# Moving the last quarter of an output product behind the next group's first tiles, in a fused attention and MLP kernel

## The chip, the cores and the metric

The kernel runs on one core of a Trainium2 chip. The time is that of the device in microseconds for one execution; the figure for a kernel is the median of several. A core has four compute engines with queues of their own, each of which runs its instructions in order: TensorE (PE in the profile), VectorE (DVE), ScalarE (ACT) and GpSimd (POOL). SP is a queue that only starts transfers. An instruction waits on semaphores that other engines and transfers raise; while it waits, everything queued behind it on its engine waits too.

## The reference

There are 8 batches of 8 heads, with 576 rows of 64 elements in each of q, k and v. k and v are averaged over 8 rows at a time, so that 72 remain; attention is then computed with all 576 rows of q. The result, 4608 rows of 512, goes through two matrices with a shrinking function between:

```
k_p, v_p = mean of k, v over groups of 8 rows
attn     = softmax(q @ k_p^T / 8) @ v_p          per batch and head
x        = attn, heads side by side              4608 x 512
h        = x @ w_in                              512 -> 2048
out      = (h - tanh(h)) @ w_out                 2048 -> 512
```

## The kernel before, in words

The order of every engine's work is written out by hand; the queues get their instructions in the order of the program's lines. PSUM, where TensorE puts its results, is addressed as eight banks of 512 fp32 values a partition, and `bank(i, shape)` names one of them. `Banks` is a rotation over some of them; a bank that is given out again makes its writer wait until the last reader has finished.

The rows are worked off in nine groups of 512. Groups 0 to 7 take the first 512 rows of each batch, group 8 the last 64 rows of all eight. For each group TensorE makes 16 tiles of h, each from four matmuls of 128x512 over `w1b`. ScalarE takes tanh of a tile into `TS`, and VectorE subtracts it and writes `Gt`. Group 0 handles tiles one by one (`mlp_h`, L580 to L582). Later groups handle tiles p and p + 8 as a pair in two neighbouring banks (`h_pair`, L616 to L622): eight matmuls, one tanh of 128x1024 at L621, one subtraction at L622.

The second product differs too. Group 0 multiplies straightforwardly (`mlp_o`, L586 to L603). For each of four row blocks `tb` it runs over the 16 tiles in four quarters `qd`, in the order of the tiles `W2_ORDER = (0, 8, 4, 12)`; after the last quarter ScalarE copies the bank to `O` (L601) and SP stores two blocks at a time. Groups 1 to 8 use a scheme with seven half-size products (`product`, L665) on sums of the blocks of `Gt` (`sum_p`, `sum_q`, `sum_d` on VectorE, L630, L635 and L640) and on sums of the blocks of `w_out`. These weight sums (`w_sum`, L648, and two ScalarE multiplications by −1 at L1015) are made once, in halves of the 8 tiles, during group 0. One of them, `b12`, is changed in place, so its half can only be made after group 0 has read those rows of `w2b`.

While group 0's output product runs, batch 1 is prepared: GpSimd adds the rows of k (`pool_k`, L247 and L252), VectorE makes `kd` (L259). TensorE turns k and q by a product with the identity (L328, L216) and makes the scores (L374), ScalarE exponentiates them (L389, L406, L407). TensorE multiplies by the values (`av_mms`, L463), VectorE divides, and TensorE turns the result into `xT` (L542). VectorE sums the rows of v and spreads them into `VB` (L270 to L309). These steps stand in a loop over 16 steps `u`, one `mlp_o` call each. Its score and turn banks rotate over banks 5, 6 and 7.

Batch 2 and later are prepared during the h tiles of the group before. GpSimd pools k and v; SP turns kd and q by transposing transfers (`k_dma_transpose`, `q_dma_transpose`, L202 and L207), and GpSimd places k (`k_place`, L360 to L362). `v_spread` copies the pooled v by three transfers. Inputs two batches ahead are loaded by SP after that.

Loads of `w2b` are issued on GpSimd's queue (L742)[...]. `after(loads, x)` adds a dependency by hand: the load of batch 2's k waits for a w2 load this way.

Of the kernel before, what the change touches and what calls it, by code (L numbers as in the profile page):

```python
# [8 lines left out]
FP32 = mybir.dt.float32  # L9
# [34 lines left out]
def kernel(  # L44
# [192 lines left out]
    def halves(n, b):  # L237
        return ((0, n),) if b < 2 else ((0, n // 2), (n // 2, n))

    def pool_k(b, eng, t0=0, t1=NT, mid=(), last=None, dep2=None):  # L240
        r = k_raw[b % 2].rearrange("p t (j d) -> p t j d", d=D)[:, t0:t1, :, :]
        if b not in kdups:
            kdups[b] = work.tile([128, NT, 2, D], BF16, name="kd", tag="kd", bufs=1)
        kd = kdups[b][:, t0:t1, :, :]
        n = t1 - t0
        for ta, tb in halves(n, b):
            eng.tensor_tensor(  # L247
                out=r[:, ta:tb, 0:4, :], in0=r[:, ta:tb, 0:4, :], in1=r[:, ta:tb, 4:8, :], op=ALU.add
            )
        for i, m in mid[0:2]:  # L250
            load_w2(i, m)
        second = eng.tensor_tensor(  # L252
            out=r[:, :, 0:2, :], in0=r[:, :, 0:2, :], in1=r[:, :, 2:4, :], op=ALU.add
        )
        if dep2 is not None:
            after([second], dep2)
        for i, m in mid[2:]:
            load_w2(i, m)
        kd_done = (last or eng).tensor_tensor(  # L259
            out=kd,  # L260
            in0=r[:, :, 0:1, :].to_broadcast([128, n, 2, D]),
            in1=r[:, :, 1:2, :].to_broadcast([128, n, 2, D]),
            op=ALU.add,
        )
        return kd_done

    def pool_v(b, eng):
        r = v_raw[b % 2].rearrange("p t (j d) -> p t j d", d=D)
        for ta, tb in halves(NT, b):
            eng.tensor_tensor(  # L270
                out=r[:, ta:tb, 0:4, :], in0=r[:, ta:tb, 0:4, :], in1=r[:, ta:tb, 4:8, :], op=ALU.add
            )
        eng.tensor_tensor(
            out=r[:, :, 0:2, :], in0=r[:, :, 0:2, :], in1=r[:, :, 2:4, :], op=ALU.add
        )
        if b < 2:
            eng.tensor_tensor(
                out=r[:, :, 0, :], in0=r[:, :, 0, :], in1=r[:, :, 1, :], op=ALU.add
            )
            v_main(VB[b % 2], r[:, :, 0:1, :], eng, 0, NM)  # L280
            return v_left(VB[b % 2], r[:, NM, 0:1, :], eng)
        if b < 4:
            eng.memset(VB[b % 2][0:G, 0:H, D:D1], float(POOL))
        vps[b] = work.tile([128, NT, D], BF16, name="vp", tag="vp", bufs=1)
        return eng.tensor_tensor(
            out=vps[b][:, :, :], in0=r[:, :, 0, :], in1=r[:, :, 1, :], op=ALU.add
        )

    vps = {}

    def v_spread(b):
        vp, vb = vps.pop(b), VB[b % 2]
        nc.sync.dma_start(out=vb[0:G, 0:H:2, 0:D], in_=vp[0:G, 0:NM, :])
        nc.sync.dma_start(out=vb[0 : 128 - G, 1:H:2, 0:D], in_=vp[G:128, 0:NM, :])
        nc.sync.dma_start(out=vb[128 - G : G, 1:H:2, 0:D], in_=vp[0 : NM * LO, NM, :])

    def v_main(vb, vs, eng, t0, t1):
        n = t1 - t0
        eng.tensor_tensor(
            out=vb[:, 2 * t0 : 2 * t1, 0:D].rearrange("p (t s) d -> p t s d", s=2),  # L300
            in0=vs[:, t0:t1, :, :].to_broadcast([128, n, 2, D]),
            in1=mask[:, 2 * t0 : 2 * t1, :]
# [280 lines left out]

    o_tiles = {}

    def mlp_o(g, tb, qd, gts, pool=None, k0=0, k1=4):  # L586
        if qd == 0:
            p, tag = pool or (ps_o, "o_ps")
            o_tiles[tb] = p.tile([128, DM], FP32, name="o_ps", tag=tag)
        o_ps = o_tiles[tb]  # L590
        i0 = W2_ORDER[qd]
        for i in range(i0 + k0, i0 + k1):
            nc.tensor.matmul(  # L593
                o_ps[:, :],
                lhsT=gts[i][:, tb * 128 : (tb + 1) * 128],
# [345 lines left out]
    ps_h.n = ps_o.n = 0  # L941
    nc.scalar.copy(out=q_bf[:QT, R, :, :], in_=t0[:QT, :, R, :])
    load_q(1, False)
    load_main(v_pairs, v_raw[1], 1, 0, NM)
    load_q_tail(1, q_raws[1], nc.scalar)
    for i in range(5):
        mlp_h_mms(0, i, 2, 4)
# [1 line left out]


    for i in range(5, NHID):
        mlp_h(0, i, gts, bank((0, 1, 2, 3, 4, 0, 1, 2, 3, 4, 2)[i - 5], [128, TG]))
        if i == 7:
            q_pe_tail(0)
        if i == 9:
            scores_tail(0)
        if i == 11:
            ps_a.n = 0
            av(0, 4, ps_any, True)
            x_dma_transpose(0, 2)  # L960
    kd1 = pool_k(1, nc.gpsimd, mid=((4, 2), (6, 2), (12, 4)), last=nc.vector)
    after([w_sum(w2s[:, 3, :, :], b21, b11, ALU.subtract, nc.gpsimd, k, k + 2) for k in (0, 2)], kd1)
    after(load_k(2), w2_dmas[3])
    load_v(2)

    def q1_cast(t, h):
        nc.scalar.copy(  # L967
            out=q_bf[:, 0:R, h : h + 4, :].rearrange("p j h d -> p h j d"),
            in_=t[:, h : h + 4, 0:R, :],
        )  # L970

    o_pools = [(ps_o, "o_ps"), (ps_o, "o_ps"), (ps_h, "hT_ps"), (ps_h, "hT_ps")]
    pend = []
    for u in range(16):
        qd, tb = u // 4, u % 4
        if u == 8:
            scores_wide(1, (3,))
            scores_ends(1)
        if qd == 2:
            for t2 in (2 * (tb % 2), 2 * (tb % 2) + 1):  # L980
                mlp_o(0, t2, qd, gts, o_pools[t2], tb // 2 * 2, tb // 2 * 2 + 2)
        else:
            mlp_o(0, tb, qd, gts, o_pools[tb])
        if u == 0:
            q1 = q_raws.pop(1)
            q1_cast(q1, 0)
        if u == 3:
            k_transpose(1, ps_any, (nc.vector.tensor_copy, nc.vector.tensor_copy))
        if u == 4:
            q_pe_transpose(1, (0, 1), "act")  # L990
            q1_cast(q1, 4)
            nc.scalar.copy(out=q_bf[:QT, R, :, :], in_=q1[:QT, :, R, :])
            load_q(2)
            w_sum(w2s[:, 1, :, :], b11, b12, ALU.add, k1=4)
            w_sum(w2s[:, 0, :, :], b11, b22, ALU.add, k1=4)
            w_sum(w2s[:, 2, :, :], b21, b22, ALU.add, k1=4)
            w_sum(b12, b22, b12, ALU.subtract, k1=4)
            v1_done = pool_v(1, nc.vector)
            after(
                [  # L1000
                    w_sum(w2s[:, 3, :, :], b21, b11, ALU.subtract, nc.gpsimd, k, k + 2)
                    for k in (4, 6)
                ],
                v1_done,
            )
            w_sum(w2s[:, 1, :, :], b11, b12, ALU.add, k0=4)
        if u in (5, 6):
            q_pe_transpose(1, (u - 3,), "act")
        if 5 <= u <= 7:
            scores_wide(1, (u - 5,))  # L1010
        if u == 6:
            q_pe_tail(1)
        if u in (9, 11):
            n = (u - 9) // 2
            nc.scalar.mul(  # L1015
                out=w2s[:, 4, 4 * n : 4 * n + 4, :], in_=b22[:, 4 * n : 4 * n + 4, :], mul=-1.0
            )
        if 11 <= u <= 14:
            x_pe_transpose(1, *pend.pop(0))
        if 9 <= u <= 12:  # L1020
            pend.append((u - 9, av(1, u - 9, ps_any, False)))
        if u == 13:
            w_sum(w2s[:, 0, :, :], b11, b22, ALU.add, k0=4)
            sums = w_sum(w2s[:, 2, :, :], b21, b22, ALU.add, k0=4)
        if u == 15:
            ps_a.n = 0
            av(1, 4, ps_any, True)
    pool_k(2, nc.gpsimd, dep2=sums)
    pool_v(2, nc.gpsimd)
    w_sum(b12, b22, b12, ALU.subtract, k0=4)  # L1030

    for g in range(1, NG):
        nb = g + 1 if g + 1 < B else None
        nn = g + 2 if g + 2 < B else None
        for p in range(NP - 1):
            c = p if g > 1 else p - 2
            if nb is not None and 0 <= c < 3:
                q_cast_part(nb, c)
            h_pair(g, p, ((2, 0, 4, 6, 0, 2, 4) if g == 1 else (0, 2, 4, 6, 0, 2, 4))[p], p % 2)
            if 3 <= p < 6:  # L1040
                sum_p(2 * p - 6, 2 * p - 4)
            if nb is not None and p == 0:
                k_dma_transpose(nb)
            if g == 1 and p == 0:
                x_dma_transpose(1, 2)
            if g > 1 and p == 0:
                store(g - 1, 2, 4, nc.gpsimd)
                store(g - 1, 0, 2, nc.gpsimd)
            if nb is not None and p == 0:
                k_place(nb, nc.gpsimd.tensor_copy)  # L1050
            if nb is not None and 0 <= c < 3:
                q_dma_transpose(nb, c)
            if nb is not None and c == 2:
                v_spread(nb)
                if nn is not None:
                    load_k(nn)
                    load_v(nn)
                    load_q(nn)
        h_one(g, NP - 1, 1, 0, 2)
        h_one(g, NP - 1, 0, 1, 3)  # L1060
        sum_p(6, 8)
        sum_q(0, 4)
        sum_q(4, 8)
        if nb is not None:
            sum_d(0, 2)
            sum_d(2, 4)
        ps_a = Banks(2, 3, 4, 5, 0, 1)
        for u in range(14):
            n, half = u // 2, u % 2
            bk, lhs, rhs = products[n]  # L1070
# [57 lines left out]
```

The softmax here doesn't subtract the row's maximum and nothing guards it: scores larger than these inputs give would overflow.

## Time and profile before

| | before |
|---|---|
| median of 8 runs | 285.69 us (285.26 to 286.61) |
| the profiled execution | 285.26 us |
| its span in the profile | 283.4 us |
| PE busy | 276.2 us, 97% |
| VectorE busy | 223.2 us, 79% |
| ScalarE busy | 157.9 us, 56% |
| GpSimd busy | 114.6 us, 40% |
| chain of waits | PE 93%, transfers 2% |

The span runs from the first to the last instruction of the profile. Where a stage is spoken of by its time, that is microseconds from the span's start. A row of the timeline shows the start, the length, the engine, the line of the kernel, the operation with what it writes and reads, how many instructions are merged in it, and in brackets how long the engine stood idle before it and what ended the idle time. A row of the busy times by stage shows the stretch and its length and then, engine by engine, busy time and number of instructions.

### The profile page before, as it was taken

The page shows a single profiled execution, that of the slowest core. Times are in us where ns is not written, and L with a number is a line of the kernel's source. Part 1 is how long each engine was busy: PE and PEld are TensorE (multiplying, and loading weights), DVE is VectorE, ACT ScalarE, POOL GpSimd, SP SyncE. Part 2 cuts the span into 40 slices and gives each one's busy share as a digit, 9 for nine tenths or more (in the row PEclk, how much of TensorE's full clock was granted, in tenths as well). Part 3 has the DMA queues.
Part 4 walks back from the last instruction along what each step waited for, and adds up shares of the span by engine and source line. Part 5 has one row for each costly group of instructions (what it writes and reads, how often), then busy time and mean ns, then how long its engine had stood idle before and what let it go on. Part 6 is the DMA issues. An engine that isn't in the chain of part 4 may idle for free.

```text
span 283.4 us, 5465 instructions
## 1 busy us (share of the span) xinstructions
PE 276.2 (97%) x2156; PEld 179.8 (63%) x2156; DVE 223.2 (79%) x338; ACT 157.9 (56%) x212; POOL 114.6 (40%) x124
## 2 busy tenths in 40 slices
PE   7999989999999999999999999999999999999994
PEld 3454445645884589448954895479547954884583
DVE  6668788979976997599859995998599839936983
ACT  4738567697527662867186718670868156215510
POOL 8600743792398029901990099009910110010000
PEclk9999999999999999999999999999999999999999
DMA  7999999984998896979788956896640440012014
GB/s 253 231 212 275 291 187 277 328 202 108 333 202 171 243 335 99 157 247 321 122 125 291 345 92 127 278 329 119 114 163 0 73 161 0 2 69 83 0 37 113
DMA packets 67253, 50.41 MB, mean 178 GB/s; under 512 B 42652, under 2 KB 56476, under 8 KB 67228
## 3 DMA queue, kind: packets, MB, share of 16 engines
q1 hardware_dynamic: 57724, 36.04, 51.3%
q0 software_dynamic: 6784, 12.06, 17.7%
q10 hardware_dynamic: 2720, 1.97, 2.4%
q8 instruction: 17, 0.28, 0.4%
q14 instruction: 8, 0.07, 0.1%
HBM read 36.70 MB, written 9.44 MB: 163 GB/s over the span
## 4 chain that ended last, share of the span: by engine, by line
PE 93%; DMA 2%; ACT 1%; DVE 1%; issue 1%; SPq 0%; ACTq 0%
PE PS L608 39%; PE PS L665 35%; PE PS L564 5%; PE PS L593 5%; PE PS L448 3%; PE PS L422 3%; DMA k_raw<-in_k_dram 2%; PE PS L463 1%; PE PS L374 1%; PE PS L216 0%; ACT qT L132 0%; PE PS L844 0%; PE PS L905 0%; PE PS L755 0%; ACT q_bf L967 0%
## 5 line engine op out<-in xcount | busy, mean ns | idle before, releaser
L608 PE MATMUL PS<-xT,w1b 128*128 128x512 bf16 (+1 forms) x504 | 98.0, 355 | 0.0
L622 DVE TENSOR_TENSOR Gt<-PS,TS 128x1024 bf16<-128x1024 f32 x56 | 68.3, 1221 | 32.8 <-ACT TS L621 32.8
L608 PEld LDWEIGHTS <-w1b 128*128 128x128 f16 x576 | 56.3, 98 | 52.7
L621 ACT ACTIVATE TS<-PS 128x1024 f32<-128x1024 f32 x56 | 57.3, 1024 | 30.0 <-PE PS L608 28.5
L709 POOL TENSOR_TENSOR m<-O,m 128x512 f32<-128x512 f32 x6 | 7.6, 1261 | 77.1 <-ACT m L707 77.1
L665 PE MATMUL PS<-w2s,Dg 128*128 128x256 f16 x256 | 30.2, 272 | 0.0
L247 POOL TENSOR_TENSOR k_raw<-k_raw 128x512 f32<-128x512 f32 (+2 forms) x13 | 21.5, 1674 | 17.8 <-DMA k_raw<-in_k_dram 17.8
L443 ACT ACTIVATE E<-PS 72x1024 bf16<-72x1024 f32 (+1 forms) x30 | 26.0, 929 | 4.1 <-PE PS L422 3.9
L665 PEld LDWEIGHTS <-Gt 128*128 128x128 bf16 x256 | 23.6, 98 | 6.8 <-issue 2.3
L665 PEld LDWEIGHTS <-P 128*128 128x128 bf16 x256 | 24.6, 98 | 3.0
L665 PEld LDWEIGHTS <-Dg 128*128 128x128 bf16 x256 | 24.6, 98 | 2.8
L630 DVE TENSOR_TENSOR P<-Gt 128x1024 bf16<-128x1024 bf16 x32 | 22.0, 688 | 0.5
L716 ACT COPY m<-PS 128x512 f32<-128x512 f32 x8 | 4.7, 585 | 29.6 <-PE PS L665 29.6
L681 POOL DMA_DIRECT2D out_dram<-O x14 | 7.7, 552 | 31.7 <-DVE O L719 29.5
L640 DVE TENSOR_TENSOR Dg<-Gt 128x1024 bf16<-128x1024 bf16 x32 | 20.4, 682 | 0.0
L270 POOL TENSOR_TENSOR v_raw<-v_raw 128x512 f32<-128x512 f32 (+1 forms) x12 | 18.2, 1541 | 0.0
L499 DVE TENSOR_TENSOR x_sb<-PS,rden 128x512 bf16<-128x512 f32 x24 | 16.6, 691 | 0.8
L665 PE MATMUL PS<-w2s,Gt 128*128 128x256 f16 x128 | 16.4, 273 | 0.0
L665 PE MATMUL PS<-w2b,P 128*128 128x256 f16 x128 | 16.3, 273 | 0.0
L1090 ACT COPY O<-PS 128x512 f32<-128x512 f32 x7 | 4.1, 585 | 21.9 <-PE PS L665 21.9
L665 PE MATMUL PS<-w2s,Q 128*128 128x256 f16 x128 | 16.3, 272 | 0.0
L665 PE MATMUL PS<-w2b,Gt 128*128 128x256 f16 x128 | 16.3, 272 | 0.0
(120 smaller groups left out, 404.4 us busy)
## 6 DMA issues: line engine op xcount, KB each, us to landing
k_raw<-in_k_dram SPq DMA_DIRECT2D x7, 1024.0 KB, 6.0
q_raw<-in_q_dram SPq DMA_DIRECT2D x7, 1024.0 KB, 10.9
v_raw<-in_v_dram SPq DMA_DIRECT2D x7, 1024.0 KB, 8.5
out_dram<-O POOLq DMA_DIRECT2D x14, 512.0 KB, 4.0
w1b<-in_moe_w_in_dram POOLq DMA_DIRECT2D x4, 512.0 KB, 14.2
w2b<-in_moe_w_out_dram POOLq DMA_DIRECT2D x3, 512.0 KB, 23.8
out_dram<-O SPq DMA_DIRECT2D x2, 512.0 KB, 6.5
k_raw<-in_k_dram SPq DMA_DIRECT2D x7, 128.0 KB, 5.9
```

Source lines behind the costliest of these rows:

```text
L247: eng.tensor_tensor(out=r[:, ta:tb, 0:4, :], in0=r[:, ta:tb, 0:4, :], in1=r[:, ta:tb, 4:8, :], op=ALU.add)
L270: eng.tensor_tensor(out=r[:, ta:tb, 0:4, :], in0=r[:, ta:tb, 0:4, :], in1=r[:, ta:tb, 4:8, :], op=ALU.add)
L443: nc.scalar.activation(out=e, in_=ps, func=ACT.Exp, scale=SCALE)
L499: nc.vector.tensor_tensor(out=x_sb[:, :, :, :], in0=ps[:, :, :, 0:D], in1=rden[:, :, :, :].to_broadcast([128, 2, 4, D]), op=ALU.mult,)
L564: nc.tensor.matmul(h_tiles[i][:, :], lhsT=w1b[:, fb, i * 128 : (i + 1) * 128], rhs=xT[g][:, :, fb, :], start=(fb == 0), stop=(fb == NFB - 1),)
L593: nc.tensor.matmul(o_ps[:, :], lhsT=gts[i][:, tb * 128 : (tb + 1) * 128], rhs=w2b[:, i, :], start=(i == 0), stop=(i == NHID - 1),)
L608: nc.tensor.matmul(dst[:, t0 * 128 : t1 * 128], lhsT=w1b[:, fb, i * 128 : (i + 1) * 128], rhs=x[:, t0:t1, fb, :], start=(fb == 0), stop=(f ...
L621: nc.scalar.activation(out=t2, in_=PS[:, b0 : b0 + 2, :], func=ACT.Tanh)
L622: nc.vector.tensor_sub(out=Gt[:, p, :, :], in0=PS[:, b0 : b0 + 2, :], in1=t2)
L630: nc.vector.tensor_tensor(out=P[:, a:b, :], in0=Gt[:, a:b, 0, :], in1=Gt[:, a:b, 1, :], op=ALU.add)
L640: return nc.vector.tensor_tensor(out=Dg[:, a:b, :, :], in0=Gt[:, a:b, :, 0:HT], in1=Gt[:, a:b, :, HT:TG], op=ALU.subtract,)
L665: nc.tensor.matmul(part(g, bk, tt), lhsT=lhs(k, slice(tt * 128, (tt + 1) * 128)), rhs=rhs[:, k, :], start=(first and k == 0 and (tt == 0 o ...
```

## The change

The 16-step loop is written out as a list, and its content is changed:

- Three quarters of group 0's output product run with batch 1's attention. The fourth quarter (tiles 12 to 15) follows group 1's h tile pairs 0 to 3, together with some of VectorE's sums and batch 2's q: its casts on ScalarE and its transposing transfers.
- Group 0's output blocks take banks 1, 2, 3 and 0; batch 1's attention rotates over banks 4, 5, 6 and 7. Group 1's pairs use banks 6, 4, 6, 4, 6, 4, 2, each with its neighbour, where they used 2, 0, 4, 6, 0, 2, 4.
- Batch 1's v is loaded and pooled in two halves and a tail; the tail is pooled during group 0's h tiles.
- The w2 loads of tiles 4 to 7 (one load instead of two) and 12 to 15 stand behind two of GpSimd's weight sums instead of among the additions for k.
- The two multiplications by −1 on ScalarE stand directly ahead of group 1's first tanh; on VectorE two weight sums stand ahead of group 1's first subtraction and one ahead of the second.
- Batch 2's inputs are loaded in the order k, q, v. Its k is placed by VectorE at pair 5 instead of GpSimd at pair 0, and its v is spread by transfers on GpSimd's queue.

The core of the diff:

```diff
-        mlp_h(0, i, gts, bank((0, 1, 2, 3, 4, 0, 1, 2, 3, 4, 2)[i - 5], [128, TG]))
+        mlp_h(0, i, gts, bank(i % 5, [128, TG]))
...
+        if i == 9:
+            pool_v1(NM, NT)
...
-    kd1 = pool_k(1, nc.gpsimd, mid=((4, 2), (6, 2), (12, 4)), last=nc.vector)
...
-    for u in range(16):
...
+    ps_a = Banks(4, 5, 6, 7)
+    q1 = q_raws.pop(1)
+    kd1 = pool_k(1, nc.gpsimd, last=nc.vector)
+    after([w_sum(w2s[:, 3, :, :], b21, b11, ALU.subtract, nc.gpsimd, k, k + 2) for k in (0, 2)], kd1)
+    load_w2(4, 4)
+    load_w2(12, 4)
+    w_sum(w2s[:, 1, :, :], b11, b12, ALU.add, k1=4)
+    mlp_o(0, 0, 0, gts)
+    q1_cast(0)
+    q1_cast(4)
+    nc.scalar.copy(out=q_bf[:QT, R, :, :], in_=q1[:QT, :, R, :])
+    mlp_o(0, 1, 0, gts)
+    mlp_o(0, 2, 0, gts)
+    k_transpose(1, ps_any, (nc.vector.tensor_copy, nc.vector.tensor_copy))
+    w_sum(w2s[:, 0, :, :], b11, b22, ALU.add, k1=4)
+    w_sum(w2s[:, 2, :, :], b21, b22, ALU.add, k1=4)
+    mlp_o(0, 3, 0, gts)
+    q_pe_transpose(1, (0, 1), "act")
+    mlp_o(0, 0, 1, gts)
+    scores_wide(1, (0,))
+    q_pe_transpose(1, (2,), "act")
+    pool_v1(0, 2)
...
+    av(1, 0, ps_any, True)
+    av(1, 1, ps_any, True)
+    mlp_o(0, 0, 2, gts)
+    turn1(0)
+    mlp_o(0, 1, 2, gts)
+    turn1(1)
+    av(1, 2, ps_any, True)
+    av(1, 3, ps_any, True)
+    mlp_o(0, 2, 2, gts)
+    turn1(2)
+    mlp_o(0, 3, 2, gts)
+    turn1(3)
+    av(1, 4, ps_any, True)
...
+    for n in range(2):
+        nc.scalar.mul(out=w2s[:, 4, 4 * n : 4 * n + 4, :], in_=b22[:, 4 * n : 4 * n + 4, :], mul=-1.0)
...
+    w_sum(w2s[:, 1, :, :], b11, b12, ALU.add, k0=4)
+    sums = w_sum(w2s[:, 0, :, :], b11, b22, ALU.add, k0=4)
+    x_dma_transpose(1, 2)
     pool_k(2, nc.gpsimd, dep2=sums)
     pool_v(2, nc.gpsimd)
...
+    def rest_of_group_0():
+        for n in range(2):
+            q_cast_part(2, n)
+            q_dma_transpose(2, n)
+        for tb in range(4):
+            mlp_o(0, tb, 3, gts)
+        sum_p(2, 4)
+        sum_q(0, 4)
+        sum_d(0, 2)
+        sum_d(2, 4)
+        w_sum(b12, b22, b12, ALU.subtract, k0=4)
...
+            if g == 1 and p == 4:
+                rest_of_group_0()
...
-            h_pair(g, p, ((2, 0, 4, 6, 0, 2, 4) if g == 1 else (0, 2, 4, 6, 0, 2, 4))[p], p % 2)
+            h_pair(g, p, ((6, 4, 6, 4, 6, 4, 2) if g == 1 else (0, 2, 4, 6, 0, 2, 4))[p], p % 2)
...
+            if g == 1 and p == 0:
+                w_sum(w2s[:, 2, :, :], b21, b22, ALU.add, k0=4)
-            if nb is not None and p == 0:
-                k_place(nb, nc.gpsimd.tensor_copy)
+            if nb is not None and p == (5 if g == 1 else 0):
+                k_place(nb, nc.vector.tensor_copy if g == 1 else nc.gpsimd.tensor_copy)
```

## The prediction

> **What bounds the kernel now.** First the head of the page, then busy time by stage.
>
> ```profile
> span 283.4 us, 5465 instructions
> ...
> PE 276.2 (97%) x2156; PEld 179.8 (63%) x2156; DVE 223.2 (79%) x338; ACT 157.9 (56%) x212; POOL 114.6 (40%) x124
> ```
> ```profile
> core 0: us, PE busy (x) PEld busy (x) DVE busy (x) ACT busy (x) POOL busy (x), PEclk, DMA share, GB/s
> 33.34:54.30 20.96, 19.80 (x154) 10.66 (x152) 17.36 (x34) 14.59 (x25) 11.12 (x10) 1.00 1.19 270
> 54.30:68.14 13.84, 13.84 (x75) 7.05 (x73) 11.82 (x14) 10.10 (x12) 10.28 (x10) 1.00 0.78 183
> 68.14:83.30 15.16, 15.16 (x170) 12.66 (x169) 14.29 (x25) 6.58 (x9) 7.39 (x5) 1.00 0.99 267
> ```
> TensorE is the bound. The change works on three stages: group 0's output product with batch 1's attention (33.34 to 54.30), group 1's h tiles (to 68.14), its products (to 83.30). Only the first has visible idle time, 20.96 − 19.80 = 1.16 us; the h stage has none. So little more than 1 us can be won here, while every new wait of PE counts in full. The waits of PE by time:
>
> ```profile
> 38.41 1.03 PE L593 MATMUL PS<-w2b,Gt 128*128 128x512 f16 x4
> 40.46 0.40 PE L216 MATMUL PS<-ident,q_bf 128*128 128x128 bf16 x4 [1.02 <-ACT q_bf L967]
> ...
> 54.14 14.00 PE L608 MATMUL PS<-xT,w1b 128*128 128x256 bf16 x72
> ```
> The wait is for ScalarE's casts of batch 1's q, and these began when q landed. ScalarE's timeline:
>
> ```profile
> 36.85 1.04 ACT L967 CAST q_bf<-q_raw 128x1024 bf16<-128x1024 f32 x1 [2.88 <-DMA q_raw<-in_q_dram]
> ...
> 45.05 0.46 ACT L407 ACTIVATE E<-PS 128x320 bf16<-128x320 f32 x1
> 45.37 1.08 ACT L1015 ACTIVATE w2s<-w2b 128x1024 f16<-128x1024 f16 x1
> ...
> 56.15 1.02 ACT L621 ACTIVATE TS<-PS 128x1024 f32<-128x1024 f32 x1 [1.57 <-PE PS L608]
> ```
> Then VectorE and GpSimd around 50 us, where the weight sums of VectorE meet GpSimd's sums over k:
>
> ```profile
> 51.89 2.90 DVE L648 TENSOR_TENSOR w2s<-w2b 128x1024 f16<-128x1024 f16 x2
> ...
> 55.55 1.47 DVE L648 TENSOR_TENSOR w2b<-w2b 128x1024 f16<-128x1024 f16 x1
> 57.20 1.23 DVE L622 TENSOR_TENSOR Gt<-PS,TS 128x1024 bf16<-128x1024 f32 x1 [0.18 <-ACT TS L621]
> ```
> ```profile
> 50.73 3.51 POOL L247 TENSOR_TENSOR k_raw<-k_raw 128x512 f32<-128x512 f32 x2 [1.33 <-DMA k_raw<-in_k_dram]
> 54.94 1.54 POOL L252 TENSOR_TENSOR k_raw<-k_raw 128x640 f32<-128x640 f32 x1 [0.70 <-DVE rden L498]
> ```
> A weight sum of 128x1024 takes 0.68 us alone (40.63 in the same timeline). Here two take 2.90: the second ends just after GpSimd's 3.51 us (at 54.24) are over. The third, at 55.55, ends 0.5 us after GpSimd's 1.54 us. They wait for each other. Last, the DMA queues from 33 to 37 us:
>
> ```profile
> q1 hardware_dynamic: 977, 1.41, 97.0%
> q0 software_dynamic: 86, 0.07, 11.0%
> ```
> While q lands, the w2 loads of the software queue move 0.07 MB of 1.49: they don't hold q up.
>
> **What the Trainium skill says.** "SBUF — State Buffer", section "Who interferes with whom": a VectorE instruction with two SBUF inputs and a GpSimd instruction that reads SBUF exclude each other for the whole instruction; one with a single SBUF input doesn't. The trace agrees: weight sums stretch, and the subtractions (one input in PSUM) stay at 1.22 to 1.23 us beside GpSimd. "DMA: Bandwidth & Descriptors", section "Anatomy of one DMA — SWDGE (gpsimd) path", gives about 2.0 us + bytes / 436,000 per us. For 1 MB read that is an estimate of 4.4 us; here the last w2 load took 11.4 us from issue to landing, behind others. So the price is a lower bound.
>
> **The change part by part.** I walk in the coordinate of the chain of waits. A quarter-product of four 128x512 matmuls costs 0.863 us (3.45 for 16), a scores tile or four 128x128 turns 0.22, six attention matmuls 0.34.
>
> *Pooling of k1.* GpSimd's second addition no longer has two w2 issues ahead of it (1.46 us) and ends about 34.3 instead of 35.73. But VectorE reaches kd only after group 0's last subtraction, about 34.75; the tail of v (four operations, some 1.3 us, from the 128x256 row of 0.42) fits into its 0.2 to 0.6 us gaps before that. kd ends near 35.6, PE arrives at 35.93 with three quarters done: no wait; the fourth ends at 37.11.
>
> *q of batch 1.* It lands at 36.85 as before. First cast to 37.80: PE waits 0.8 for the turns. ScalarE now does the second cast and the tail (0.95 + 0.60) before it evacuates the turns; the first evacuation ends 39.9, while PE is free at 39.25: 0.73. ScalarE then runs without a gap: evacuations and exponentials at a pitch of 0.48 to 0.5, the last end at 44.9. PE has 44.6; the first attention block waits 0.35 for that bank. v1 needs 2 x 1.7 us on VectorE, three weight sums and the KB copies between, over near 43.5: not last. The fourth block's second half takes the bank that the second turn's evacuation frees at 48.5: 0.2. In all 2.1 us of waits, where before had 1.16 and some short ones for the three banks of its scores (one exponential, 0.61 us, stands on its chain at 43.61), which a fourth bank removes. With twelve quarters done PE starts group 1 at 51.2; the like moment before was 54.30 − 3.45 = 50.85. **Cost +0.35**, bounds −0.3 and +1.
>
> *w2 loads.* Their issue moves on GpSimd's queue from 32.7 to about 38.1, behind two weight sums (2.26 us) that wait for kd. PE needs rows 4 to 7 at 45.7. In the trace the queue alone moves 0.20 MB per us (43 to 45 us), so 0.5 MB are 2.6 us. Issued by 38.8, and started only after the lull that the trace shows in both queues (23 GB/s from 39.5 to 41.3, while the x transpose issued at 31.7 has still to land), they land near 44. I take 0, hidden behind the attention stage with 1.7 us to spare; bounds 0 and 4.5 (11.4 us from 38.8). SP's loads for batch 2 hang on this landing: k2 at about 51 as now (issue at 43.68, landing 50.73), then q2 and v2 in the other order, q2 wanted at 61, v2 at 58.
>
> *Group 1's first four pairs.* This is the main cost. The pairs alternate between two pairs of banks (6,7 and 4,5) where before there were four. A pair's matmuls are 1.73 us; its banks come free after tanh (1.02) and subtraction (1.22) with about 0.1 for each handover. Pair 0 ends 52.95, pair 1 54.68; pair 2 then needs pair 0's subtraction. On ScalarE the two L1015 multiplications (2 x 0.97 pitch), formerly at 45, are now queued directly ahead of the first tanh: 51.5 to 53.45, so tanh 0 ends 54.45. On VectorE two weight sums are queued ahead of the first subtraction, from 52.2 on. Without collision the subtraction ends 55.65: PE waits 1.0, and little at pair 3: 1.1. But GpSimd's k2 additions run from 51.0 to about 54.5 in that very place: one weight sum slips in, the other ends at 55.2, the subtraction at 56.4: PE waits 1.77. The third weight sum, before the second subtraction, meets GpSimd's next addition (55.2 to 56.75), and pair 3 waits 0.4 more. Sum 2.2; 2.7 if both weight sums are caught. I take **+2.0**, bounds 1.1 and 2.7.
>
> *The last quarter after pair 3.* Sixteen matmuls (3.45) move with it, no cost; they hide pairs 4 and 5's bank waits and ScalarE's four O copies and three q casts (2 x 1.0 + 0.6). The last tanh of these is 0.4 late, caught up by pair 6. VectorE gets five sums and b12 (6 x 0.65) here; two of them meet GpSimd's v2 (until 64): pair 4's subtraction ends near 69, not 68.
>
> *The place of k2 on VectorE:* the same three copies from PSUM took 0.45, 0.40 and 0.22, so at most 1.07; at least 0.3. I take 0.6. They stand before pair 6's subtraction, which ends 72.7 or, without collisions, 71.9. The second score block of the product stage needs its banks at 71.8: **+0.5**, bounds 0.1 and 0.95.
>
> *SP and POOL queues:* q2's transposes and the O stores come some 12 us later (stores about 65 to 67.5). The rows of O are written again near 76; a store took 6.5 us to land, so 2 us remain. v2's spread goes to GpSimd's queue after its vp, about 64 to 67, wanted by the attention blocks after 75. No cost.
>
> Sum: 0.35 + 2.0 + 0.5 = 2.85. The profiled execution is 285.26 (span 283.4 + 1.86 around it), giving 288.1; the median of the eight runs is 285.69, giving **288.5**.
>
> **The rivals.** *No collision and short waits:* k2 lands after the weight sums. Cost 0.2 + 1.1 + 0.1 = 1.4: 287.1. For it: a microsecond moves it; against: both landings repeat today's. *w2 late:* rows 4 to 7 land at 47 instead of 44; PE stands 1.3 more: 289.8, or 292 at the bound. For it: the 11.4 us; against: less queued ahead. *On the other side:* q1 lands 1.5 us sooner, at 35.3. ScalarE's row then begins 1.5 us earlier, the 2.1 us of waits in the first stage vanish, and with 1.1 us at the banks and 0.1 after the sum is 0.35 − 2.1 + 1.2 = −0.55: 285.1. It decides from about 1 us of earlier landing. Against: the queue row above, q already had the engines to itself.
>
> **How the numbers follow.** Forecast 0.62, short waits 0.14, w2 late 0.14, q sooner 0.10. A measurement tells about 0.2% (0.57 us) from no change. Half of the last case is faster by more, half lies within it, and so does a fifth of the short-waits case: faster 0.05, same 0.08, slower 0.87. The range runs from half a microsecond below short waits to late w2 with the bank bound: 286.6 to 290.6.
>
> **What would show it.** Right: PE idle of 1 to 2.5 us ahead of pair 2 (between 54 and 57), released by VectorE's subtraction; weight sums longer than 0.68 beside GpSimd; ScalarE's two multiplications directly ahead of the first tanh; PE waits on q casts and evacuations near 37.5 and 39.5. Wrong: PE without a gap there, q casts starting well before 36.8, PE waiting for a w2 landing at 46, or DVE waiting for an O store at 76.

## The result and the profile after

| | before | after |
|---|---|---|
| median | 285.59 us of 32 runs (284.91 to 287.35) | 292.19 us of 11 runs (289.49 to 296.46) |
| the profiled execution | 285.26 us | 292.19 us |
| its span | 283.4 us | 290.4 us |
| start of group 1's h tiles, with all of group 0's product but the fourth quarter done | 50.69 us (54.14 less 3.45) | 51.18 us |
| start of group 1's products | 67.97 us | 71.07 us |
| start of group 2's h tiles | 83.16 us | 90.00 us |
| from there to the end of the span | 200.2 us | 200.4 us |

The starts are those of the rows in TensorE's timeline. The prediction's 54.30, 68.14 and 83.30 are the ends of the rows before them, which overlap the starts by some 0.15 us.

The changed kernel is slower. The ratio is 1.0185, with a 95% interval in brackets here and below, [1.0161, 1.0209], against 1.0098 for the predicted 288.5 us. The ratios leave out executions more than 1.5% above the fastest of their kernel, so this one stands for some 290.9 us and the full median lies higher. The direction was right, the time is outside the range. The times also scatter, as those before do not: three lie at 289.5 to 290.5, three near 292, five at 294.9 to 296.5.

The profiled span grew by 7.0 us, most of it between 51 and 90 us. 0.5 were there when group 1's tiles began. The h stage took 19.89 us from start to start instead of 17.28 (13.83 and the moved quarter's 3.45): 2.6. The product stage took 18.9 instead of 15.2: 3.7. First the head of the changed kernel's page:

```profile
span 290.4 us, 5464 instructions
...
PE 278.6 (96%) x2156; PEld 180.6 (62%) x2156; DVE 226.5 (78%) x340; ACT 157.8 (54%) x212; POOL 115.1 (40%) x123
...
PE 80%; DVE 8%; DMA 6%; ACT 3%; issue 1%; ACTq 0%
```

TensorE has as many instructions as before (x2156), yet was busy 278.6 us instead of 276.2: matmuls have become slower. And VectorE now holds 8% of the chain of waits. TensorE's timeline shows both; the number in brackets is its idle time before the row and what ended it.

```profile
51.18 3.69 PE L610 MATMUL PS<-xT,w1b 128*128 128x256 bf16 x24
56.66 1.89 PE L610 MATMUL PS<-xT,w1b 128*128 128x512 bf16 x8 [1.80 <-DVE Gt L624]
58.89 1.89 PE L610 MATMUL PS<-xT,w1b 128*128 128x512 bf16 x8 [0.34 <-DVE Gt L624]
...
71.07 1.05 PE L667 MATMUL PS<-w2s,Gt 128*128 128x256 f16 x8
73.06 0.76 PE L425 MATMUL PS<-qT,KB 64*72 64x512 bf16 x2 [0.94 <-DVE KB L363]
74.67 0.64 PE L425 MATMUL PS<-qT,KB 64*72 64x512 bf16 x2 [0.85 <-DVE Gt L624]
75.24 1.89 PE L667 MATMUL PS<-w2s,Gt 128*128 128x256 f16 x8
```

The first two waits are those of the bank pairs, 1.80 and 0.34. The next two are in the product stage: group 1's scores of batch 2 wait for k's placement, then for pair 6's subtraction. The last row is the same work as the row at 71.07 (eight matmuls of 128x256) and took 1.89 us instead of 1.05. The busy times by stretch tell why (columns as in the prediction; the third figure from the end is the clock that TensorE was granted):

```profile
71.00:73.00 2.00, 1.12 (x9) 0.70 (x8) 1.97 (x4) 1.78 (x3) 0.00 (x0) 1.00 0.96 351
73.00:75.00 2.00, 1.09 (x4) 0.35 (x4) 1.94 (x5) 1.34 (x2) 0.00 (x0) 0.88 1.05 327
75.00:77.00 2.00, 2.00 (x11) 1.27 (x10) 1.97 (x4) 1.02 (x1) 0.00 (x0) 0.50 1.01 349
...
71.10:90.10 19.00, 17.20 (x170) 13.61 (x170) 14.83 (x26) 8.31 (x11) 7.37 (x5) 0.91 0.75 213
```

In steps of 0.2 us the clock falls at 74.5, before the second wait is over, and is back at 77.9: 3.4 us at 0.50. In the whole stage 170 matmuls cost 17.20 us, where before 170 cost 15.16. Of these 2.0 us the clock makes some 1.7 (half of 3.4). The rest is an estimate of what starting again after the two waits costs. With 1.8 us of waits that is the loss of the stage, to 0.1 us.

Who was late? VectorE is without a gap from 71 to 77. Its timeline goes back to GpSimd, and GpSimd's to a transfer:

```profile
63.01 3.80 DVE L632 TENSOR_TENSOR P<-Gt 128x1024 bf16<-128x1024 bf16 x2
66.73 1.34 DVE L637 TENSOR_TENSOR Q<-Gt 128x1024 bf16<-128x1024 bf16 x1
...
69.80 2.34 DVE L624 TENSOR_TENSOR Gt<-PS,TS 128x1024 bf16<-128x1024 f32 x2
```
```profile
61.27 3.04 POOL L266 TENSOR_TENSOR v_raw<-v_raw 128x512 f32<-128x512 f32 x2 [2.16 <-DMA v_raw<-in_v_dram]
64.39 1.87 POOL L269 TENSOR_TENSOR v_raw<-v_raw 128x640 f32<-128x640 f32 x1
```

In the kernel before, the same additions began without a wait:

```profile
58.38 3.05 POOL L270 TENSOR_TENSOR v_raw<-v_raw 128x512 f32<-128x512 f32 x2
61.52 1.54 POOL L273 TENSOR_TENSOR v_raw<-v_raw 128x640 f32<-128x640 f32 x1
```

There they met VectorE's subtractions, which have one input in PSUM and were not stretched (1.22 to 1.23 us). Now GpSimd stood 2.16 us until v of batch 2 had landed, at 61.2. Its operations on v, which ended at 67.5, therefore fell on the first three of VectorE's six sums; the six took 6.8 us (63.01 to 69.80) instead of six times 0.65. Behind the sums on VectorE's queue stood the subtractions of pairs 4 and 5, one more sum, k's placement (three copies, 0.6 us) and pair 6's subtraction, which ended at 74.6.

### The profile page after: what moved, and what is told of

Read it like the earlier page. It is cut to its first block, busy times and chain, and to the rows that moved or that the text cites. A ratio compares the mean times of both kernels' runs of the same rounds, so it can differ in the third digit from the quotient of the medians.

```text
span 290.4 us, 5464 instructions
## 1 busy us (share of the span) xinstructions
PE 278.6 (96%) x2156; PEld 180.6 (62%) x2156; DVE 226.5 (78%) x340; ACT 157.8 (54%) x212; POOL 115.1 (40%) x123
## 4 chain that ended last, share of the span: by engine, by line
PE 80%; DVE 8%; DMA 6%; ACT 3%; issue 1%; ACTq 0%
PE PS L667 34%; PE PS L610 34%; DMA q_raw<-in_q_dram 6%; PE PS L451 3%; PE PS L425 3%; DVE Gt L624 2%; PE PS L595 2%; DVE P L632 2%; DVE w2s L650 1%; PE PS L757 1%; PE PS L466 1%; PE PS L377 1%; PE PS L216 1%; PE PS L567 1%; ACT L783 0%
## 5 line engine op out<-in xcount | busy, mean ns | idle before, releaser
L632 DVE TENSOR_TENSOR P<-Gt 128x1024 bf16<-128x1024 bf16 x32 | 24.4, 765 | 0.5
L502 DVE TENSOR_TENSOR x_sb<-PS,rden 128x512 bf16<-128x512 f32 x28 | 19.4, 691 | 1.0
L667 PE MATMUL PS<-w2s,Gt 128*128 128x256 f16 x128 | 17.3, 282 | 0.0
```

The costliest lines, as they stand in the source:

```text
L502: nc.vector.tensor_tensor(out=x_sb[:, :, :, :], in0=ps[:, :, :, 0:D], in1=rden[:, :, :, :].to_broadcast([128, 2, 4, D]), op=ALU.mult,)
L632: nc.vector.tensor_tensor(out=P[:, a:b, :], in0=Gt[:, a:b, 0, :], in1=Gt[:, a:b, 1, :], op=ALU.add)
L667: nc.tensor.matmul(part(g, bk, tt), lhsT=lhs(k, slice(tt * 128, (tt + 1) * 128)), rhs=rhs[:, k, :], start=(first and k == 0 and (tt == 0 o ...
```

## Experiments

Theory A is that the new order k, q, v of batch 2's loads is what makes v late, and with it VectorE's sums and the product stage. Against it stood that the sums themselves, taken forward by the change, are too much (B); that the waits at group 1's first pairs are what matters (C); that the three copies which place k are the cause (D); and that the clock is a loss of its own. A further theory, E, came out of the first four kernels' traces. In all experiments the change is relative to the changed kernel, except in the two on the kernel before. Every one had four executions or more; the medians of before beside them were 285.69, 286.32 and 285.86 us.

### v of batch 2 ahead of q

```diff
-    load_q(2)
     load_v(2)
+    load_q(2)
     av(1, 0, ps_any, True)
```

> The changed kernel with batch 2's v loaded before its q, as the kernel before had it. Theory A (late v2): v2 landed at 61.2 us because it stands third in SP's queue, so GpSimd's v additions ran from 61.3 to 67.5 and caught VectorE's five sums after pair 3 (6.2 us in place of 3.9). With v second, GpSimd should go on to v near 59.1 without a wait and end about 65; VectorE's five sums take 4.5 to 5.5 us, PE's waits in the product stage fall from 1.8 to about 0.5 to 1.0 us, and the time falls by 1 to 3 us (more if the clock also stays up). Theory B (too much two-input work on VectorE, whatever GpSimd does): less than 0.5 us of change. Theory C (the wait at the two bank pairs is what matters): no change, and the clock still falls.

Measured: 291.09 us (288.84 to 293.03), ratio 1.0184 [1.0128, 1.0241]. The profiled execution took 288.84, 3.35 less than that of the changed kernel. TensorE, VectorE and GpSimd in it:

```profile
72.81 0.41 PE L425 MATMUL PS<-qT,KB 64*72 64x512 bf16 x2 [0.41 <-DVE Gt L624]
```
```profile
63.07 2.54 DVE L632 TENSOR_TENSOR P<-Gt 128x1024 bf16<-128x1024 bf16 x2
...
67.95 2.34 DVE L624 TENSOR_TENSOR Gt<-PS,TS 128x1024 bf16<-128x1024 f32 x2
```
```profile
59.12 3.05 POOL L266 TENSOR_TENSOR v_raw<-v_raw 128x512 f32<-128x512 f32 x2
```

Within the profile theory A holds, against B (less than 0.5 us) and C (the waits at the pairs are the same, 1.82 and 0.34): GpSimd's additions of v began at 59.12 us without a wait, the six sums took 4.9, one wait of 0.41 is left in the product stage and the clock stays at 1.00. The mean clock was 0.999 or above in all four executions, where six of the eleven of the changed kernel have 0.983 to 0.994. But the median moved by only 1.1 us, and the times still scatter by 4, now at full clock. So something else, outside this order and the clock, acts in some executions and not in others.

### The sums put back, and the weight sums taken forward

The first of two kernels leaves three of VectorE's five sums where they were, in the product stage; the second moves the weight sums and multiplications ahead of group 1's pairs into VectorE's and ScalarE's idle time beside the attention.

```diff
         sum_p(2, 4)
-        sum_q(0, 4)
-        sum_d(0, 2)
-        sum_d(2, 4)
...
-        if g > 1:
-            sum_q(0, 4)
+        sum_q(0, 4)
...
-        if nb is not None and g > 1:
+        if nb is not None:
```

> The changed kernel with three of VectorE's sums (Q of the first half and both D of the first half) put back behind group 1's last tile, where the kernel before has them. Theory A and B both expect the subtraction of pair 4 to start as soon as its tanh ends (near 67.1, not 69.8), the last pair's tanh not to wait, and the 1.8 us of PE waits in the product stage to fall to 0.2 or less; 2 us less, and up to 4 us less if the clock stays up too. If the two waits come from the three copies that place k (theory D), they stay above 0.6 us.

```diff
     mlp_o(0, 3, 1, gts)
+    neg(0)
+    w_sum(w2s[:, 1, :, :], b11, b12, ALU.add, k0=4)
...
     turn1(1)
+    neg(1)
+    sums = w_sum(w2s[:, 0, :, :], b11, b22, ALU.add, k0=4)
...
     turn1(2)
+    w_sum(w2s[:, 2, :, :], b21, b22, ALU.add, k0=4)
```

> The changed kernel with the three VectorE weight sums and the two ScalarE multiplications moved from in front of group 1's first tanh and subtractions into idle time of both engines in the attention stage. The prediction's step says that they and GpSimd's k2 additions delay pair 0's subtraction to 56.6: PE's 2.1 us of waits at pairs 2 and 3 should fall to 0.4 to 0.8, what two bank pairs cost by themselves (4.2 us a round against 3.46). Rival: the two bank pairs alone make the wait; then it stays above 1.5 us. The product stage should keep its waits; if its clock fall comes from pairs 2 and 3, it should go (2 us less besides).

Sums back: 289.63 us (288.1 to 290.51), 1.013 [1.0095, 1.0166]. The wait for k's placement was gone, the one of 0.85 for pair 6's subtraction stayed, because the two sums left took 4.16 us beside GpSimd's late v. The expectation of almost no wait was missed in that. Weight sums forward: 292.87 us (289.62 to 295.69), 1.0169 [1.0126, 1.0213]. TensorE in that kernel:

```profile
55.74 3.61 PE L610 MATMUL PS<-xT,w1b 128*128 128x512 bf16 x16 [0.70 <-DVE Gt L624]
...
70.15 1.05 PE L667 MATMUL PS<-w2s,Gt 128*128 128x256 f16 x8 [0.44 <-DVE Gt L624]
72.14 0.76 PE L425 MATMUL PS<-qT,KB 64*72 64x512 bf16 x2 [0.95 <-DVE KB L363]
73.75 0.41 PE L425 MATMUL PS<-qT,KB 64*72 64x512 bf16 x2 [0.85 <-DVE Gt L624]
```

The waits of the bank pairs fell from 2.14 to 0.70 us: 0.7 is the price of the two bank pairs alone, 1.4 that of what was queued ahead. Part of it was lost again: TensorE came sooner to a VectorE that was as late as ever, and waited there longer (2.24 instead of 1.79 us), so that the profiled execution, at 291.54 us, is only 0.65 faster. The clock fell here too, from 74.3 to 77.7 us; so the fall does not need the long waits at the pairs.

These traces also showed something that no expectation had asked for. In the kernel with the sums put back, VectorE and GpSimd near 30 us:

```profile
30.34 3.12 DVE L312 TENSOR_TENSOR VB<-v_raw,mask 128x256 bf16<-128x256 f32 x1
...
37.80 0.81 DVE L255 TENSOR_TENSOR kd<-k_raw 128x640 bf16<-128x640 f32 x1
```
```profile
30.28 2.89 POOL L247 TENSOR_TENSOR k_raw<-k_raw 128x1280 f32<-128x1280 f32 x1 [15.79 <-DMA k_raw<-in_k_dram]
```

Compare the changed kernel's own profile, VectorE and then GpSimd:

```profile
29.59 0.43 DVE L312 TENSOR_TENSOR VB<-v_raw,mask 128x256 bf16<-128x256 f32 x1
...
34.53 0.81 DVE L255 TENSOR_TENSOR kd<-k_raw 128x640 bf16<-128x640 f32 x1
```
```profile
29.87 2.91 POOL L247 TENSOR_TENSOR k_raw<-k_raw 128x1280 f32<-128x1280 f32 x1 [16.44 <-DMA k_raw<-in_k_dram]
```

And the kernel with v ahead of q, in the same order:

```profile
29.77 0.43 DVE L312 TENSOR_TENSOR VB<-v_raw,mask 128x256 bf16<-128x256 f32 x1
```
```profile
29.80 3.14 POOL L247 TENSOR_TENSOR k_raw<-k_raw 128x1280 f32<-128x1280 f32 x1 [16.22 <-DMA k_raw<-in_k_dram]
```

The last operation of v's tail has two inputs in SBUF. In the changed kernel's profile it began 0.28 us ahead of GpSimd's first addition for k and took 0.43 us, and with v ahead of q a lead of 0.03 us was enough. With the sums put back it began 0.06 us after the addition and stood until that was over: 3.12 us. `kd` was ready 3.3 us later, and group 1's tiles began at 53.16 us instead of 51.18. This is theory E: the tail and k's addition race. It isn't that k lands early. In the losing execution GpSimd began 0.41 us later than in the changed kernel's profile, but VectorE, which follows its own queue, came 0.75 later. Which of the two starts first decides it in each execution.

### The wait filled

Nine matmuls of zeros, which are no part of the computation and whose result is not used, stand in TensorE's queue where the product stage waits:

```diff
+                    if g == 1:
+                        warm_pe(9, b0=C2)
```

> The changed kernel with nine matmuls on zeros (1.94 us) put where PE waits 1.8 us for the first scores of group 1's product stage; they write a bank that is free there. Nothing else changes. If the fall of TensorE's granted clock to 0.5 between 74 and 78 us follows from PE's idle time there, the clock stays at 1.00 in that stage, it takes about 17 us in place of 19, and the runs spread less: about 289.5 in place of 290 to 296. If the clock falls for another reason (idle time at pair 2), nothing is won.

Measured: 291.37 us (290.14 to 293.76), 1.0183 [1.0143, 1.0222]. The clock stayed at 0.997 or above in all four executions, and at 1.00 from 71 to 80 us of the profiled one. So with TensorE kept at work there, no execution shows the fall. But the filler costs time too, and the median is near 291 and not 289.5. The profiled execution had lost the race (3.00 us for the tail's last operation, group 1 from 54.06 us), so its stage stands under other waits than the changed kernel's, and this kernel alone doesn't price the clock.

### The tail pooled later, and where it always collides

```diff
-        if i == 9:
-            pool_v1(NM, NT)
...
     q_pe_transpose(1, (2,), "act")
+    pool_v1(NM, NT)
     pool_v1(0, 2)
```

> The changed kernel with the four VectorE operations on the tail of batch 1's v moved from group 0's h tiles to the place just before v's first half. Theory E (the tail races with GpSimd): GpSimd's first addition for k1 (2.9 us) begins about 29.9 us, 0.3 us after the last of the four has begun in a lucky execution; where k1 lands first, that last one takes 3.1 us in place of 0.43, and the attention stage is 2 to 3 us late (kd ends 38.6 in place of 35.3). Without the race no execution should show kd after 36, the slowest of the four times should be near the fastest, and the median 1 to 2 us lower. It costs up to 0.4 us at the first attention block, since v is ready 1.3 us later. Rival: the spread comes from the fall of the clock in the product stage alone; then the spread stays.

```diff
-        if i == 9:
+        if i == 10:
             pool_v1(NM, NT)
```

> The changed kernel with the tail of batch 1's v one h tile later (after tile 10 in place of tile 9), so that GpSimd's first addition for k1 always has begun by its last operation. Theory E: every execution has kd at about 38.5, PE starts group 1 near 53 to 54 in place of 51.2, and the time is at or above the slow end of the changed kernel unless the later phases absorb some of it. Rival (no exclusion, the tail is cheap): nothing changes.

Later, out of the race: 290.68 us (289.55 to 293.79), 1.0174 [1.0123, 1.0224]. There was no collision, but the scatter stayed, and with it granted clocks from 0.988 to 1.00: the small scatter that was expected was missed, and the clock's fall scatters the times by itself. GpSimd's additions of v in this kernel:

```profile
59.68 3.04 POOL L266 TENSOR_TENSOR v_raw<-v_raw 128x512 f32<-128x512 f32 x2
```

This limits theory A. v is still third in the queue, yet GpSimd went on to it without a wait; the six sums took 5.0 us, 0.49 was left of the waits in the product stage, and the clock did not fall there in this execution. Of the six profiled kernels with v third, GpSimd waited for v in four (0.91 to 2.53 us); of the four with v second, in none. So the order makes it likely, and not certain, that v is late.

One tile later, into the collision: 294.9 us (293.96 to 295.95), 1.0307 [1.0268, 1.0346]. VectorE, then TensorE, then the stretches in this kernel:

```profile
30.52 4.62 DVE L282 TENSOR_TENSOR v_raw<-v_raw 128x256 f32<-128x256 f32 x3
...
39.34 0.82 DVE L255 TENSOR_TENSOR kd<-k_raw 128x640 bf16<-128x640 f32 x1
```
```profile
36.25 1.02 PE L595 MATMUL PS<-w2b,Gt 128*128 128x512 f16 x4 [2.35 <-DVE Gt L580]
```
```profile
34.00:36.00 2.00, 0.00 (x0) 0.00 (x0) 1.93 (x4) 0.00 (x0) 0.73 (x1) 1.00 1.08 385
...
38.00:40.00 2.00, 2.00 (x6) 0.76 (x5) 2.00 (x4) 1.28 (x2) 0.00 (x0) 0.50 0.20 45
```

The three additions took 4.62 us instead of 1.00, group 0's last tiles came late, TensorE stood 2.35 us, its clock fell to 0.50, and group 1 began at 55.39, later than the 53 to 54 that were expected. A second fall, from 61.6 to 65.0 us, came after a wait of 2.23 us at pair 2. All four executions took more than 293.9 us. So the race has a price of its own and can take the clock with it.

### Only the bank pairs, and only the tail, in the kernel before

```diff
-            h_pair(g, p, ((2, 0, 4, 6, 0, 2, 4) if g == 1 else (0, 2, 4, 6, 0, 2, 4))[p], p % 2)
+            h_pair(g, p, ((6, 4, 6, 4, 6, 4, 2) if g == 1 else (0, 2, 4, 6, 0, 2, 4))[p], p % 2)
```

> The kernel before with one part of the change alone: group 1's pairs on the banks 6, 4, 6, 4, 6, 4, 2 in place of 2, 0, 4, 6, 0, 2, 4. In the kernel before b12 stands ahead of the first subtraction, and ScalarE's three q casts stand between its tanhs, so with two pairs of banks PE waits about 0.6 us at pair 2 and once a cast for pairs 3 to 5: 1.5 to 3 us in all, 287.2 to 288.7. Rival (tanh and subtraction of a pair fit beside the other pair's 1.73 us): no wait, 285.7.

```diff
+        if i == 9:
+            pool_v1(NM, NT)
...
-            v1_done = pool_v(1, nc.vector)
+            v1_done = pool_v1(0, NM)
```

> The kernel before with another part of the change alone: the tail of batch 1's v is pooled by VectorE after group 0's tile 9 (four operations moved, nothing added). Theory E: an execution in which GpSimd's first addition for k1 starts before the last of them has PE 1 to 3 us late at the k turns, the others are at 285.7 or a little less, since v is ready sooner: the runs fall into two groups or spread over 2 us. Rival: all runs within 0.3 us of the kernel before.

Bank pairs: 288.17 us (287.87 to 288.81), 1.0088 [1.006, 1.0116], with little scatter and as expected. TensorE waited 0.69 and 0.63 us for subtractions, and 1.09 at pair 1, whose banks 4 and 5 batch 1's end rows still held. That last wait belongs to the old rotation of the attention's banks; in the changed kernel pair 1 doesn't wait. Tail: 285.77, 289.98, 290.05 and 285.55 us. Two executions are as fast as the kernel before, two 4.3 us slower, with granted clocks of 0.993 and 0.994 against 0.997 and 0.998. The profiled execution (285.77) had won the race:

```profile
29.65 0.43 DVE L316 TENSOR_TENSOR VB<-v_raw,mask 128x256 bf16<-128x256 f32 x1
```
```profile
29.84 2.98 POOL L247 TENSOR_TENSOR k_raw<-k_raw 128x1280 f32<-128x1280 f32 x1 [16.37 <-DMA k_raw<-in_k_dram]
```

One edit on an otherwise untouched kernel makes the two groups. That the two near 290 us lost the race is inferred, since neither was profiled.

### Both mended, and what remains

```diff
-    load_q(2)
     load_v(2)
+    load_q(2)
...
-        if i == 9:
-            pool_v1(NM, NT)
...
+    pool_v1(NM, NT)
     pool_v1(0, 2)
```

> The changed kernel with only two edits: v of batch 2 before its q, and v's tail moved out of the race. The waits at pairs 2 and 3 (2 us) stay, those of the product stage should be 0.5 us or less and the clock at 0.997 or more; with 1 us in the attention stage the time is 288.5 to 289.5 in all runs. If the clock's fall comes from the waits at the pairs, it shows here (below 0.995).

These two edits together: 289.33 us (288.64 to 290.2), 1.0127 [1.0095, 1.0159], every clock at 0.999 or above. The waits of 1.80 and 0.34 us at pairs 2 and 3 are still there, one of 0.40 in the product stage. The scatter is 1.6 us instead of 7, and the time lies inside the predicted range. It also shows that 1.80 us of waiting at one place did not cost the clock. The two edits and their combinations:

| | v third, behind q | v second, ahead of q |
|---|---|---|
| tail during group 0's h tiles | 292.19 us (289.49 to 296.46), clock 0.983 to 0.999 | 291.09 us (288.84 to 293.03), clock 0.999 or above |
| tail later | 290.68 us (289.55 to 293.79), clock 0.988 to 1.00 | 289.33 us (288.64 to 290.2), clock 0.999 or above |

The order of the loads goes with the clock, and the tail with the scatter that is left at full clock.

```diff
+    neg(0)
+    w_sum(w2s[:, 1, :, :], b11, b12, ALU.add, k0=4)
...
-        sum_q(0, 4)
-        sum_d(0, 2)
-        sum_d(2, 4)
```

> The changed kernel with the four edits together: v of batch 2 loaded before its q, VectorE's three sums put back into the product stage, the weight sums and multiplications moved into idle time, v's tail moved. If the causes add up as the walk says, what is left over the kernel before is about 0.3 to 0.7 us in the attention stage, 0.7 us at the two bank pairs and 0.2 in the product stage, with the clock up: 286.9 to 287.5. If something else costs as much, it stays above 288.5.

With the sums put back and the weight sums forward as well, whose full edits are above: 287.78 us (287.26 to 290.71), 1.007 [1.0043, 1.0097]. 286.9 to 287.5 was expected. TensorE's waits at the pairs are 0.70 us, in the product stage 0.18. The attention stage costs 1.3 us (group 1 began at 51.95) where 0.3 to 0.7 was expected, and TensorE waits there 0.58 for `VB`, which the later tail holds up on VectorE. One of the nine executions (290.71) had a clock of 0.993: the fall has become rare, not impossible.

The same with one row block of the last quarter left beside the attention and three behind pair 1 instead of four behind pair 3; the row blocks beside the attention are each drawn one place forward for it, and two weight sums stand in other places:

```diff
-            if g == 1 and p == 4:
-                rest_of_group_0()
+            if g == 1 and p == 2:
+                for tb in range(1, 4):
+                    mlp_o(0, tb, 3, gts)
```

> The mended kernel with the last quarter's matmuls moved again: one row block beside batch 1's attention, three behind pair 1 in place of pair 3, so that they cover the bank wait of pair 2; and one more quarter-product ahead of the q turns and ahead of the first attention block, where PE waits 1.5 us. The walk expects no bank wait at pairs 2 and 3 (0.7 us less than the mended one) and 0.9 us less in the attention stage: 285.0 to 286.0, level with the kernel before or up to 0.3% faster. Rival: the w2 rows 4 to 7, now wanted at 43.9, come too late and PE waits for them; then 286.5 or more.

Measured: 287.78 us (287.38 to 290.55), 1.0079 [1.0046, 1.0111], where 285 to 286 was expected. The wait for banks went from pair 2 to pair 4 (0.65 us), and the attention stage got waits for `x_sb` (0.5) and a w2 load (0.4). No arrangement that was run beats the kernel before.

## Why the prediction was wrong, step by step

**The sum.** It gave 288.1 us for a profiled execution; 292.19 was measured, 4.1 more. With v ahead of q it is 288.84; the 0.7 that remains lies in the attention stage (0.1) and at the first pairs (0.6), inside their bounds. So one failed term makes the profiled execution late. A second one shows only in other executions.

**Attention stage, +0.35: right.** Group 1 began at 51.18 us, as predicted; from row start to row start (50.69) that is 0.49 later. TensorE waited 0.7 for the casts of q (0.8 predicted), 0.5 for the first evacuation (0.73), 0.3 for the first attention block (0.35).

**w2 loads, 0: right.** The load of k that hangs on them was issued at 43.98 us, where 44 was estimated, and no wait of TensorE names w2.

**The first four pairs, +2.0: right.** 1.80 and 0.34 us of idle time, where 1.77 and 0.4 were worked out; counted from start to start the stage grew by 2.6, since each break also cost some 0.2 us that the brackets don't show. The weight sums forward split the term into 0.7 for the banks and 1.4 for what stands ahead. It agrees with the Trainium skill, "SBUF — State Buffer", section "Who interferes with whom": VectorE's two weight sums took 3.25 us beside GpSimd's 3.48 over k.

**Batch 2's v on SP's queue, priced at nothing: wrong, and this is the step that failed.** Under the w2 loads the prediction says that q and v come "in the other order, q2 wanted at 61, v2 at 58", and puts no cost to it. It had worked out when v is wanted, and not when it would land. Under the last quarter it then keeps the old times of v, "until 64", has two sums stretched, and lets pair 4's subtraction end near 69. In the profiled execution v landed at 61.2 us, GpSimd stood 2.16 and was at v until 67.5. The lateness didn't reach TensorE as a wait for v, which is why it looked free: the attention wants v only after 75 us. It reached it by way of the lock, the mutual exclusion of VectorE and GpSimd that the prediction describes. Three sums were caught (the six took 6.8 us instead of 3.9), pair 4's subtraction began at 69.80 and ended at 71.0, and the subtraction of pair 6 ended at 74.6, not 72.7. v ahead of q brings the predicted times back: GpSimd is done with v at 65.1, pair 4's subtraction ends at 69.2 and pair 6's at 72.8, and 0.41 us of wait is left in the product stage, which is the **+0.5** of that term as predicted. k's placement took 0.6 us, the value taken.

**Not in the working at all: the clock.** Two waits of 0.94 and 0.85 us within 2.6 us went with 3.4 us at 0.50, about 1.7 us lost. The Trainium skill, "TensorE: Matmul & The Clock Gate", section "Part 1: The HAM clock gate", has a half rate that a TensorE without enough work falls to; the 0.50 agrees with it. The rule of its section "Why this matters for your kernels", no gaps above about 3 us, doesn't cover this case: the trace has a fall after gaps below 1 us each, and none after one of 1.80 in the same execution. Nearer is "A second HAM failure mode: psum-queue depth-cycling", on a kernel whose many short idle times let the rate fall; it gives no length for them. Why the 1.80 at pair 2 is harmless the runs don't settle. Nor do they give a threshold: in the 3.4 us ahead of the fall TensorE had stood for 1.6 us in all, less than the 1.80.

**v's tail, "fits into its 0.2 to 0.6 us gaps": a second step that failed, without trace in the profiled execution.** The gaps were counted and the length of the operations (1.3 us), but not what GpSimd reads at the time, though the prediction itself had priced that lock at the pairs. The profiled execution won the race, which was luck. The profiles in which it was lost (3.12 and 3.00 us for the last operation), the tail in the kernel before (285.6 or 290.0 us) and the tail one tile later (294.9) show that it is a race and what it costs. It fits the groups in the times of the changed kernel: won with full clock 289.5 to 290.5, one of the two troubles near 292, both above 294. This last assignment is inferred from the clocks and from the experiments; each execution's own race was seen only where a profile was taken. One more execution on record, which is not among the eleven, took 290.19 us at a clock of 0.992 and doesn't fit it.

**The rivals.** Short waits, late w2 and an earlier q didn't occur: GpSimd's additions for k ran beside the weight sums, w2 was in time, and the first cast's wait stayed.

## What to carry to other kernels

A transfer that is wanted late can still be late for a lock: when loads change places in a queue, follow the engine that consumes each one and see which two-input operations of VectorE it will now run beside. An operation that is slipped into gaps must be held against what GpSimd reads at that moment, to less than a tenth of a microsecond if the two can start together; a single profile shows only one outcome, so a kernel whose times fall in groups should be profiled again before its profile is believed. And a term of the sum that is a wait of TensorE may have a second one behind it, the clock.

## What of the hardware was not expected

- Who starts first decides a lock, by hundredths of a microsecond, and VectorE, when it loses, stands until GpSimd's instruction is over: the same operation took 0.43 us when it began 0.28 or 0.03 us before GpSimd's addition, and 3.12 us when it began 0.06 us after.
- Four falls of the clock to 0.50 can be read in the traces: at 74.5 us in the changed kernel, at 74.3 with the weight sums forward, at 37.7 and 61.6 with the tail one tile later. Each lasted 3.4 us and so cost about 1.7. Two idle times of 0.94 and 0.85 us close together, and of 0.95 and 0.85, went with a fall, as did waits of 2.35 and 2.23 us. One of 1.80 us did not (0.999 or above in all four executions with v ahead of q and the tail later).
- VectorE placed k in copies of 0.22, 0.22 and 0.19 us over 64 partitions, SBUF to SBUF. In the kernel before, GpSimd took 0.44, 0.37 and 0.24 for those of batch 3 (from 90.20 us). For the first copy of batch 2, at 63.95 us, it took 0.88, beside one of VectorE's sums.
